# Groups of unused products between the first TensorE stages, and another order of polar work and decoding, in a linear-attention and two-layer expert kernel

## The chip, the cores and the metric

The kernel runs on one core of one Trainium2 chip. The metric is the time of one execution in device microseconds (us). TensorE (PE in the rows), VectorE (DVE), ScalarE (ACT), GpSimd (POOL) and the DMA queues each have a queue of their own, worked off in order. They meet at semaphores.

## What is computed

Three parts follow each other: a linear attention with a complex decay, a feed-forward layer with a leaky slope, and a layer of eight experts of which each token takes one.

```python
def _attn_ref(q, k, v, a_re, a_im):          # 4 batches, 8 heads, 768 steps, 48 channels
    mag = np.sqrt(a_re * a_re + a_im * a_im)
    scale = np.minimum(mag, 0.999) / (mag + 1e-06)
    ...
    for t in range(S):
        S_re, S_im = ar * S_re - ai * S_im + kv, ar * S_im + ai * S_re
        y[:, :, t] = np.einsum('bhd,bhde->bhe', q[:, :, t], S_re)

def _moe_ref(x, w_in, w_out, alpha):          # 3072 tokens, 384 -> 2048 -> 384
    h = x @ w_in
    g = np.maximum(h, 0.0) + alpha * np.minimum(h, 0.0)
    return g @ w_out

def _moe2_ref(x, modality_id, w_gate, modality_bias, w1, w2):
    e_idx = np.argmax(x @ w_gate + modality_bias[modality_id], axis=1)
    ...
    out[mask] = gate_w[mask, None] * (np.maximum(x[mask] @ w1[e], 0.0) @ w2[e])
```

## The kernel before

The 768 steps are cut into 6 chunks of 128, so that with 4 batches there are 24 pieces (`k`). Two pieces make a unit of 256 tokens (`u`), 12 units in all.

For each pair of pieces the polar work (`polar_group`, lines 673 to 789) turns the decays into magnitude and angle. VectorE and ScalarE share it: squares, reciprocal roots, an arctangent, running products and sums (line 737), sine and cosine, and at its end the tile `z`. The first pair runs as two halves, the second one (pieces 2 and 3) in one on tiles named `p`. `z` is written to memory and read back in another layout as `qk` (`bounce`, `bounce_back`). Then `attn` computes the products `pa`, masks them on VectorE into `at`, turns the keys (`pk`, copied by ScalarE into `ks`), forms `py` and the state sum `pu`, and splits `py` into a high part on ScalarE (`t`, `xt`, line 831) and a low part on VectorE (line 832). Two small DMAs per piece complete `xt`.

The feed-forward weights come as 64-bit numbers. `decode` (lines 613, 616, 619) puts them together on VectorE, three instructions for each of 16 blocks. ScalarE makes the high part of a block (line 566), VectorE the low part `w` (line 567), TensorE turns the block (`pl`, line 571) and ScalarE copies that to `wT`. `weights_gate` multiplies `wT` with the gate's weights (`og`, line 585), which ScalarE copies out as `of`.

`moe1` runs 8 steps for each unit. A step has 18 products into `ph` (lines 876 to 879), ScalarE's `n` (line 884), VectorE's `n` (line 886), ScalarE's `gh` (line 889), VectorE's `gl` (line 864), and 12 products into `acc` (line 919). From unit 2 on, each unit's polar work and attention are spread over the steps of the unit before.

The order of the work before and between the first steps is written out by hand in two texts. `START` holds what comes before the first step, `TURN` what each of the first 15 steps adds. In them `x` and `y` stand for one polar instruction of piece 0 or 1, `q` for one of pieces 2 and 3, `p` for one of the third pair; `A`, `a`, `B`, `C` for one part of the attention of piece 0, of piece 1, of unit 1 and of unit 2; `D` for the decoding of two blocks and `F` for what follows it; `b` and `c` for the bounces; `r` makes later decoding stand behind the last VectorE instruction so far; `w` is a group of 28 products that nothing reads (`warm`, line 180), issued while the first bounce is under way. Between `<` and `>` the VectorE instructions are chained. A scheduler then places the instructions of each engine, so that the texts set the queues but don't equal them.

Of the kernel before, what the change touches and what calls it, by code (L numbers as in the profile page):

```python
# [11 lines left out]
F32 = mybir.dt.float32  # L12
# [7 lines left out]
B, H, S, D = 4, 8, 768, 48  # L20
# [7 lines left out]
F2 = 8  # L28
# [6 lines left out]
NEARLY = 4  # L35
NFINAL = 3
NTRIP = 1
START = 'x2 y x2 y2 x y3 x2 y x2 y3 < x3 y x y x < x3 > x y > x2 < x4 y x b y6 r y5 < c w A2 a A > a A a2 < > q12 D q12 r q7 F q5 D d'
TURN = ('B', 'D2 > B F2 B2 D B3', 'B L D F3', '', 'D', 'D F p', '', 'F', '< p2 < p > p3', 'p3 < p3 > p > p11', 'p7', '', 'p4 < C3', 'C2 p C3 >2 s >', '')
GHB = 3  # L40
ATB = 2
LEAD = 3
# [12 lines left out]
WL = 5  # L55
WN = 28
BB = 1
OT = "xg"
OB = 4
HD = 4  # L60
# [38 lines left out]
class Emit:  # L99
    def __init__(self, ctx, tc, aps):  # L100
        self.ctx, self.tc, self.nc = ctx, tc, tc.nc
        self.__dict__.update(aps)
        self.ahead, self.loaded = {}, None
        self.raws, self.vs, self.zs, self.zd, self.queue = {}, {}, {}, {}, None
        self.behind = None
        self.nwarm = 0
        self.paced = self.sine = None
        self.pacing = True
        self.scattered = []
        self.free = {"pa": ["pa0", "pa1"], "pq": ["pq0", "pq1"]}  # L110
# [14 lines left out]
    def consts(self):  # L125
        nc, cp = self.nc, self.cp
        self.tiny = cp.tile([128, 1], F32, name="tiny")
        nc.vector.memset(self.tiny, 1e-25)
        warm = cp.tile([128, 1], F32, name="warm")
        nc.scalar.activation(warm, self.tiny, AF.Abs_reciprocal_sqrt)  # L130
        self.trig = cp.tile([128, 1], F32, name="trig")
        self.ident = cp.tile([128, 128], F32, name="ident")
# [42 lines left out]
    def warm(self, x, n):  # L175

        pt = self.ps.tile([128, 512], F32, name=f"warm{self.nwarm}", tag="acc", bufs=2)
        self.nwarm += 1
        for _ in range(n):
            self.nc.tensor.matmul(pt[:, :128], self.ident, x, start=True, stop=True)  # L180

    def route_consts(self):
        nc, cp, mp = self.nc, self.cp, self.mp
# [213 lines left out]
    def unit_out(self, nm, nt, ids, gate, acc):  # L397
        nc, qp = self.nc, self.qp
        for t in range(nt):
            ot = qp.tile([128, XW], F32, name=f"ot{nm}_{t}", tag=OT, bufs=OB)[:, :DM]  # L400
            nc.vector.tensor_scalar(ot, acc[t], gate[:, t:t + 1], None, ALU.mult)
# [273 lines left out]
    def polar_group(self, ks, wa, wq, work, inline):  # L675
# [90 lines left out]
        for i, k in enumerate(ks):  # L766
# [11 lines left out]
            if inline:  # L778
                self.bounce(k)
                if not BB:  # L780
                    self.bounce_back(k)
        if inline and BB:
            for k in ks:
# [376 lines left out]
def body(ctx, tc, aps):  # L1160
    em = Emit(ctx, tc, aps)
# [4 lines left out]
    def polar(*ks):  # L1166
        st = third if ks[0] == 4 else em.polar(ks)
        for k in ks:
            em.load_v(k)
        yield  # L1170
        yield from em.polar_run(st, 0, len(ks), True)
        yield

    def run(gen, n=1000):
        for _ in range(n):
            v = 1
            while v == 1:
                v = next(gen, 0)
            if v == 0:
                return  # L1180

    def op(gen):

        while next(gen, 1) != 1:
            pass
# [12 lines left out]
    def attn_unit(u):  # L1198
        xts[u] = em.wp.tile([128, 3, 2, 256], F32R, name=f"xt{u}", tag="xt", bufs=XB)
        for k in (2 * u, 2 * u + 1):  # L1200
            yield from em.attn(k, xts[u])
# [17 lines left out]
    def chained(c):  # L1219

        done = len(tc.nc.cur_bb.bb.instructions)
        with tc.issue_after(chain[0]) if chain[0] else nullcontext():
            step(c)
        for i in tc.nc.cur_bb.bb.instructions[done:]:
            if i.engine == mybir.EngineType.DVE:
                chain[0] = i

    def step(c):

        if c in "xyqp":  # L1230
            op(gens[c])
        elif c in "AaB":
            next(gens[c], 0)
        elif c == "w":
            em.warm(zs0[WZ][:, 0, 0, :CH], WN)
        elif c == "b":
            zs0[0] = em.zs[0]
            em.bounce(0)
            if BX:
                em.bounce_back(0)  # L1240
        elif c == "c":
            zs0[1] = em.zs[1]
            em.bounce(1)
            if not BX:
                em.bounce_back(0)
            em.bounce_back(1)
            em.weights_load(range(WL, 9 + W9))
            for k in (2, 3):
                em.load_v(k)
        elif c == "r":  # L1250
            em.behind = em.last
        elif c == "s":
            em.behind = None
        elif c == "C":
            run(gens["C"], 1)
        elif c == "L":
            for k in ("pa", "pq"):
                em.free[k].remove(k + "1")
        elif c == "d":
            em.weights_load(range(9 + W9, NFC))  # L1260
            third.extend(em.polar((4, 5)))
        elif c in "De":
            if not parts or parts[-1][1] == 0:
                if fc[0] == NFC:
                    return
                parts.append([em.weights_part(fc[0], fc[0] + 1), 1])
                fc[0] += 2
            while True:
                parts[-1][1] = next(parts[-1][0], 0) or 0
                if c == "e" or parts[-1][1] == 0:  # L1270
                    break
        elif c == "F":
            if parts:
                next(parts.pop(0)[0], 0)
# [3 lines left out]
    def steps(text):  # L1278

        for part in re.findall("([^0-9 ]+)([0-9]*)", text):  # L1280
            for c in part[0] * int(part[1] or 1):
                if c in "<>":
                    link[0] = c == "<"
                else:
                    with em.behind_turn() if c in PT else nullcontext():
                        (chained if link[0] else step)(c)

    gens["p"], gens["C"] = polar(4, 5), attn_unit(2)
    steps(START)
    jobs, later = {}, {}  # L1290
# [21 lines left out]

    for g, text in enumerate(TURN):
        first, _, then = text.partition("/")
# [74 lines left out]
    tab2, trip, n = tabs["f"]  # L1389
# [83 lines left out]
```

## Time and profile before

| | us |
|---|---|
| median of 3 runs | 902.87 |
| lowest and highest | 901.29 and 905.11 |
| the profiled execution, its own time | 901.13 |
| its span, from the first to the last instruction | 899.4 |
| TensorE, busy | 822.4 (91%) |
| VectorE, busy | 673.3 (75%) |
| ScalarE, busy | 466.6 (52%) |
| mean granted TensorE clock | 0.964 |

A time of the profile counts from the first instruction. A granted clock of 1.00 is TensorE at 2.4 GHz, 0.50 is 1.2 GHz. A row of the timeline gives the start, the time taken, the engine, the line and operation, the tiles written and read, the count, and in brackets how long the engine had been idle before it and what ended that. A row that takes longer than the step to the next row overlaps it, since an engine's instructions are pipelined.

### The profile page before, as it was taken

How to read it: one execution, taken by the hardware profiler on the slowest of the kernel's cores; microseconds unless marked ns; L12 is line 12 of the kernel's file. 1: busy time of each engine (PE TensorE's matmuls, PEld its weight loads, DVE VectorE, ACT ScalarE, POOL GpSimd, SP SyncE). 2: the span in 40 equal slices, each digit the busy share in tenths (PEclk: the TensorE clock that was granted, in tenths of full speed). 3: DMA queues.
4: the chain of work that ended last, by engine and by line, in shares of the span. 5: the costliest groups of instructions: out<-in, count | busy, mean ns of one | idle time of the engine just before them, and what ended most of it. 6: DMA issues, size and time to landing. Idle time of an engine off the chain costs nothing.

```text
span 899.4 us, 16054 instructions
## 1 busy us (share of the span) xinstructions
PE 822.4 (91%) x5949; PEld 783.4 (87%) x5949; DVE 673.3 (75%) x1419; ACT 466.6 (52%) x871; POOL 204.8 (23%) x204
## 2 busy tenths in 40 slices
PE   0769898999899999999999999899999999999893
PEld 0658898989899998999999999899988888999893
DVE  7999788999986978788888889355644755656851
ACT  7645266757564746565656464223343444455550
POOL 2000221021211121212121121000332543534650
PEclk9978698999999999999999999899999999999997
DMA  8869101645548235353626271500355477567650
GB/s 334 252 202 316 42 3 36 180 162 149 145 104 204 72 88 142 94 129 104 151 89 169 69 190 46 132 24 8 123 173 140 154 231 259 190 236 268 193 176 20
DMA packets 63591, 130.37 MB, mean 145 GB/s; under 512 B 10456, under 2 KB 39656, under 8 KB 63504
## 3 DMA queue, kind: packets, MB, share of 16 engines
q1 hardware_dynamic: 59536, 119.49, 44.4%
q0 software_dynamic: 3968, 9.77, 3.3%
q8 instruction: 49, 0.80, 0.4%
q14 instruction: 38, 0.31, 0.1%
HBM read 98.17 MB, written 28.91 MB: 141 GB/s over the span
## 4 chain that ended last, share of the span: by engine, by line
PE 61%; DVE 16%; DMA 8%; issue 4%; ACT 3%; POOL 1%; SPq 0%; DVEq 0%; ACTq 0%; POOLq 0%
PE acc L919 14%; PE a2s L505 6%; PE ph L876 6%; PE ph L879 5%; PE ph L877 5%; PE pa L807 4%; DMA zd<-z 3%; DMA qk<-zd 3%; PE p2s L490 2%; PE p2s L486 2%; PE p2s L487 2%; DVE n L886 2%; PE py L825 2%; PE pu L839 2%; PE og L585 1%
## 5 line engine op out<-in xcount | busy, mean ns | idle before, releaser
L876 PE MATMUL ph<-xt,w 128*128 128x256 f32 x576 | 157.0, 300 | 6.7 <-DVE n L886 4.2
L919 PE MATMUL acc<-w,gh 128*128 128x392 f32 x768 | 159.0, 345 | 0.4 <-ACT gh L889 0.4
L877 PE MATMUL ph<-xt,w 128*128 128x256 f32 x576 | 151.2, 290 | 0.0
L919 PEld LDWEIGHTS acc<-w,gh 128*128 128x128 f32 x768 | 134.0, 190 | 1.2 <-ACT gh L889 0.7
L876 PEld LDWEIGHTS ph<-xt,w 128*128 128x128 f32 x576 | 113.6, 197 | 8.8 <-DVE n L886 4.5
L886 DVE SCALAR_TENSOR_TENSOR n<-n,al,ph 128x256 f32<-128x256 f32 x192 | 83.9, 472 | 43.4 <-ACT n L884 42.9
L877 PEld LDWEIGHTS ph<-xt,w 128*128 128x128 f32 x576 | 113.8, 198 | 0.5 <-issue 0.5
L879 PE MATMUL ph<-xt,w 128*128 128x256 f32 x576 | 103.2, 289 | 0.0
L884 ACT ACTIVATE n<-ph 128x512 f32<-128x512 f32 x96 | 57.0, 593 | 74.8 <-PE ph L879 73.7
L864 DVE TENSOR_TENSOR gl<-n,gh 128x512 fp32r<-128x512 f32 x96 | 66.6, 694 | 33.5 <-ACT gh L889 33.4
L919 PE MATMUL acc<-w,gl 128*128 128x392 f32 x384 | 89.5, 348 | 0.0
L889 ACT CAST gh<-n 128x512 fp32r<-128x512 f32 x96 | 59.3, 617 | 57.2 <-DVE n L886 54.7
L879 PEld LDWEIGHTS ph<-xt,w 128*128 128x128 f32 x576 | 85.2, 196 | 0.0
L268 POOL DMA_INDIRECT tbl<-tok,ix x24 | 27.4, 1141 | 200.8 <-DVE ix L266 190.2
L919 PEld LDWEIGHTS acc<-w,gl 128*128 128x128 f32 x384 | 70.7, 193 | 0.3 <-issue 0.3
L807 PE MATMUL pa<-qk 96*128 96x128 f32 x384 | 54.0, 285 | 10.6 <-DMA qk<-zd 9.8
L807 PEld LDWEIGHTS pa<-qk 96*128 96x128 f32 x384 | 50.5, 197 | 13.3 <-issue 7.5
L494 DVE SCALAR_TENSOR_TENSOR hls<-p2s,hhs 128x512 fp32r<-128x512 f32 x32 | 22.0, 688 | 32.8 <-ACT hhs L493 32.8
L505 PE MATMUL a2s<-whs,hhs 128*128 128x384 f32 x128 | 43.8, 342 | 0.0
L505 PE MATMUL a2s<-wls,hhs 128*128 128x384 f32 x128 | 43.5, 340 | 0.0
L825 PE MATMUL py<-at,v 128*64 128x128 f32 x384 | 42.5, 289 | 0.3 <-DVE xt L832 0.3
L474 ACT CAST whs<-wrs 128x768 fp32r<-128x768 f32 x32 | 26.3, 834 | 30.8 <-PE a2s L505 17.0
(361 smaller groups left out, 1883.0 us busy)
## 6 DMA issues: line engine op xcount, KB each, us to landing
zd<-z SPq DMA_DIRECT2D x24, 771.0 KB, 4.7
qk<-zd SPq DMA_DIRECT2D x24, 771.0 KB, 7.2
wraw<-in_w_io_dram SPq DMA_DIRECT2D x16, 768.0 KB, 12.1
wrs<-in_wcat_dram SPq DMA_DIRECT2D x32, 384.0 KB, 4.2
ck<-in_w_io_dram SPq DMA_DIRECT2D x16, 768.0 KB, 5.0
wrf<-in_wcat_dram SPq DMA_DIRECT2D x24, 384.0 KB, 3.7
wa<-in_pa__dram SPq DMA_DIRECT2D x10, 768.0 KB, 4.8
wq<-in_pq__dram SPq DMA_DIRECT2D x10, 768.0 KB, 8.6
```

Source lines behind the costliest of these rows:

```text
L268: nc.gpsimd.indirect_dma_start(out=self.tbl, out_offset=bass.IndirectOffsetOnAxis(ap=ix, axis=0), in_=self.tok[:, c, b, :], in_offset=None ...
L505: nc.tensor.matmul(acc[t], x[:, 128 * t:128 * t + 128], w[:, DM:], start=(f == 0 and x is hh and w is wh), stop=(last and x is hl))
L807: nc.tensor.matmul(pa[:, i, :], kt[:, h, :], qt[:, h, :CH], start=True, stop=True)
L825: nc.tensor.matmul(o, v[:, h * D:h * D + 64], ats[g][:, i, :], start=True, stop=(c == 0))
L864: return engine.tensor_tensor(gl, nf, gh.bitcast(F32), ALU.subtract).ins
L876: nc.tensor.matmul(ph[:, i, :], w1(fc, 0, c), xt[:, c, 0, :], start=(c == 0), stop=False)
L877: nc.tensor.matmul(ph[:, i, :], w1(fc, 0, c), xt[:, c, 1, :], start=False, stop=False)
L879: last = nc.tensor.matmul(ph[:, i, :], w1(fc, 1, c), xt[:, c, 0, :], start=False, stop=(c == 2)).ins
L884: nc.scalar.activation(nf, ph, AF.Relu, scale=-1.0)
L886: paced = nc.vector.scalar_tensor_tensor(nf[:, i, :], nf[:, i, :], self.al1[:, 2 * p + i:2 * p + i + 1], ph[:, i, :], ALU.mult, ALU.add).ins
L889: copy = nc.scalar.copy(gh, nf).ins
L919: nc.tensor.matmul(acc[t][:, :XW], x[:, i, 128 * t:128 * t + 128], self.w[2 * p + i][:, h, DM:], start=(p == i == h == 0 and x is gh), sto ...
```

## The change

Two texts and one small function. `START` and `TURN` are written anew, and a step `f` is added: `fill` issues four products of the identity with itself into a buffer of the `acc` kind, directly behind the last TensorE instruction so far. Nothing reads them. `START` holds 11 such steps, that is 44 products. In the new `START` the second pair's polar work (`q`) begins between the halves of piece 1 and goes on in longer runs, the first decoding (`D`) stands behind most of it, and `r` stands behind the first part of the attention. In `TURN` the parts `D`, `F` and `p` of the first steps are regrouped, and the last two of unit 2's parts `C` move.

```diff
-START = 'x2 y x2 y2 x y3 x2 y x2 y3 < x3 y x y x < x3 > x y > x2 < x4 y x b y6 r y5 < c w A2 a A > a A a2 < > q12 D q12 r q7 F q5 D d'
-TURN = ('B', 'D2 > B F2 B2 D B3', 'B L D F3', '', 'D', 'D F p', '', 'F', '< p2 < p > p3', 'p3 < p3 > p > p11', 'p7', '', 'p4 < C3', 'C2 p C3 >2 s >', '')
+START = 'x3 y2 x3 y3 x y x y x y3 < x3 y2 x < x4 > x2 y > x3 < x y2 < x2 q b y10 c w A2 a A > r f a A f a f a < > q f2 q8 f2 q5 D F q3 r f q2 f q9 f q3 f q4 D d'
+TURN = ('B', 'D2 B F2 B > B2 D F B', 'B2 D F2 L', '', 'D', 'D F p', '', 'p3 F', '<2 p > p2', 'p > p3 < p3 > p11', 'p7', '', 'p4 < C3', 'C3 >2 s >', 'C p C')
...
+FN = 4
...
+    def fill(self, n):
+        if self.filled is None:
+            self.filled = self.ps.tile([128, 512], F32, name="fill", tag="acc", bufs=2)
+        last = [i for i in self.nc.cur_bb.bb.instructions if i.engine == mybir.EngineType.PE][-1]
+        with self.tc.issue_after(last):
+            for _ in range(n):
+                self.nc.tensor.matmul(self.filled[:, :128], self.ident, self.ident, start=True, stop=True)
...
+        elif c == "f":
+            em.fill(FN)
```

What the queues look like is seen in three places. On TensorE, at the end of piece 1's attention, where `pl` turns the first two decoded blocks and `ph_0` is the first step of unit 0, before:

```order
L825 MATMUL py_365<-at_0_316,v_135 64x128 x4
L825 MATMUL py_365<-at_1_346,v_135 64x128 x4
L571 MATMUL pl_447<-ident,wf_415 128x128 x3
L571 MATMUL pl_438<-ident,wf_414 128x128 x3
L876 MATMUL ph_0_514<-xt_151,w_435 128x256
```

and now:

```order
L836 MATMUL py_377<-at_1_354,v_135 64x128 x4
L191 MATMUL fill<-ident 128x128 x4
L850 MATMUL pu_397<-v_135,ks_1_361 96x48 x4
L191 MATMUL fill<-ident 128x128 x16
L582 MATMUL pl_455<-ident,wf_444 128x128 x3
L582 MATMUL pl_464<-ident,wf_445 128x128 x3
L191 MATMUL fill<-ident 128x128 x16
L887 MATMUL ph_0_559<-xt_151,w_452 128x256
```

Two blocks of 16 fills stand before and behind the two `pl`; the other 12 fills are in groups of 1 to 4 between the parts of the attention.

On VectorE, where piece 3's attention (`at_1`, `t_3`, `xt`, `state`) meets the decoding of the eighth pair of blocks, before:

```order
L809 TENSOR_TENSOR at_1_668<-pa_1_663,mask 128x512
L567 TENSOR_TENSOR w_751<-wf_560,w_751 128x768
L567 TENSOR_TENSOR w_759<-wf_561,w_759 128x768
L832 TENSOR_TENSOR t_3_686<-py_677,t_3_686 128x128
L613 TENSOR_SCALAR wf_743<-wraw_483 128x768
L613 TENSOR_SCALAR wf_744<-wraw_485 128x768
L832 TENSOR_TENSOR xt_499<-py_677,xt_499 128x3x128
L616 SCALAR_TENSOR_TENSOR wf_743<-wraw_483,wf_743 128x768
L616 SCALAR_TENSOR_TENSOR wf_744<-wraw_485,wf_744 128x768
L843 TENSOR_TENSOR state<-pu_733,qk_473 96x384
L619 SCALAR_TENSOR_TENSOR wf_743<-wraw_483,wf_743 128x768
```

and now:

```order
L820 TENSOR_TENSOR at_1_729<-pa_1_724,mask 128x512
L897 SCALAR_TENSOR_TENSOR n_1_770<-n_1_770,al_109,ph_1_738 128x256 x2
L875 TENSOR_TENSOR gl_0_776<-n_0_591,gh_0_595 128x512
L854 TENSOR_TENSOR state<-pu_794,qk_518 96x384
L843 TENSOR_TENSOR t_3_787<-py_778,t_3_787 128x128
L624 TENSOR_SCALAR wf_804<-wraw_528 128x768
L624 TENSOR_SCALAR wf_805<-wraw_530 128x768
L843 TENSOR_TENSOR xt_544<-py_778,xt_544 128x3x128
L627 SCALAR_TENSOR_TENSOR wf_804<-wraw_528,wf_804 128x768
L627 SCALAR_TENSOR_TENSOR wf_805<-wraw_530,wf_805 128x768
L630 SCALAR_TENSOR_TENSOR wf_804<-wraw_528,wf_804 128x768
```

`n_1` and `gl_0`, which stood ahead of `at_1`, stand behind it, the two `w` have gone ahead of it, and `state` has moved ahead of `t_3`. From the four `w` behind the last rows on, VectorE's queue is the same as before.

On ScalarE, where piece 2's `t_2` and `xt` are split off, before:

```order
L884 ACTIVATE n_1_725<-ph_1_693 128x512
L831 CAST t_2_624<-py_615 128x128
L566 CAST w_759<-wf_561 128x768
L831 CAST xt_499<-py_615 128x3x128
L587 COPY of_719<-og_712 128x16
```

and now:

```order
L895 ACTIVATE n_1_770<-ph_1_738 128x512
L577 CAST w_708<-wf_605 128x768
L577 CAST w_716<-wf_606 128x768
L842 CAST t_2_669<-py_660 128x128
L842 CAST xt_544<-py_660 128x3x128
```

Two `w` now stand between `n_1` and `t_2`. Lines after the change count 2 to 11 more than before; the first step of unit 1 (`ph_0` on `xt_499`, now `xt_544`) and all behind it on TensorE stand in the same order as before.

## Rows read from the trace of the kernel before

**Rows 1.** The page's part 1: busy us, share of the span, instructions of each engine.

```profile
PE 822.4 (91%) x5949; PEld 783.4 (87%) x5949; DVE 673.3 (75%) x1419; ACT 466.6 (52%) x871; POOL 204.8 (23%) x204
```

**Rows 2.** Busy time by stretch: stretch, us, each engine's busy us (instructions), TensorE's granted clock, DMA share, GB/s.

```profile
36.00:48.00 12.00, 10.25 (x103) 9.11 (x103) 12.00 (x17) 7.80 (x13) 0.00 (x0) 1.00 1.04 359
48.00:56.00 8.00, 2.54 (x23) 1.70 (x20) 8.00 (x12) 4.48 (x13) 0.00 (x0) 0.77 0.31 100
56.00:66.00 10.00, 7.29 (x40) 6.77 (x40) 10.00 (x19) 2.46 (x7) 0.36 (x2) 0.67 0.69 216
...
86.00:95.00 9.00, 8.87 (x50) 7.54 (x51) 5.41 (x10) 3.04 (x7) 0.00 (x0) 0.62 0.14 42
95.00:110.00 15.00, 12.51 (x67) 11.43 (x66) 10.49 (x17) 4.38 (x12) 2.84 (x11) 0.67 0.25 52
110.00:130.00 20.00, 19.43 (x144) 19.11 (x144) 17.91 (x29) 11.70 (x23) 6.04 (x8) 0.99 0.05 11
```

**Rows 3.** Timeline of VectorE.

```profile
28.43 0.95 DVE L687 TENSOR_TENSOR p<-p,p 128x768 f32<-128x768 f32 x1
...
59.88 1.02 DVE L613 TENSOR_SCALAR wf<-wraw 128x768 int32<-128x768 int32 x2
...
70.81 0.69 DVE L809 TENSOR_TENSOR at<-pa,mask 128x512 f32<-128x512 f32 x1 [0.37 <-PE pa L807]
...
88.52 0.69 DVE L809 TENSOR_TENSOR at<-pa,mask 128x512 f32<-128x512 f32 x1 [1.78 <-PE pa L807]
...
92.75 0.29 DVE L832 TENSOR_TENSOR t<-py,t 128x128 fp32r<-128x128 f32 x1 [1.81 <-ACT t L831]
...
97.27 0.55 DVE L843 TENSOR_TENSOR state<-pu,qk 96x384 f32<-96x384 f32 x1 [1.09 <-PE pu L839]
...
99.47 3.56 DVE L567 TENSOR_TENSOR w<-wf,w 128x768 fp32r<-128x768 f32 x4
...
104.33 0.55 DVE L613 TENSOR_SCALAR wf<-wraw 128x768 int32<-128x768 int32 x1
108.30 0.99 DVE L864 TENSOR_TENSOR gl<-n,gh 128x512 fp32r<-128x512 f32 x1 [3.42 <-ACT gh L889]
```

**Rows 4.** Timeline of TensorE.

```profile
27.73 8.45 PE L180 MATMUL warm<-z,ident 128*128 128x128 f32 x56 [27.73 <-DVE z L776]
...
52.89 0.87 PE L571 MATMUL pl<-ident,wf 128*128 128x128 f32 x3 [3.50 <-DVE xt L832]
55.72 0.55 PE L876 MATMUL ph<-xt,w 128*128 128x256 f32 x1 [1.95 <-DMA xt<-t]
...
59.45 1.40 PE L585 MATMUL og<-wg,wT 128*128 128x8 f32 x12
63.56 0.90 PE L571 MATMUL pl<-ident,wf 128*128 128x128 f32 x3 [2.71 <-DVE wf L619]
...
67.19 2.69 PE L919 MATMUL acc<-w,gh 128*128 128x392 f32 x8 [0.45 <-ACT gh L889]
...
83.89 0.55 PE L571 MATMUL pl<-ident,wf 128*128 128x128 f32 x3 [0.57 <-ACT wT L575]
...
101.38 2.73 PE L585 MATMUL og<-wg,wT 128*128 128x8 f32 x12 [0.57 <-ACT wT L575]
104.43 2.73 PE L585 MATMUL og<-wg,wT 128*128 128x8 f32 x12 [0.32 <-ACT of L587]
107.01 0.56 PE L876 MATMUL ph<-xt,w 128*128 128x256 f32 x1
...
148.97 0.58 PE L876 MATMUL ph<-xt,w 128*128 128x256 f32 x1 [4.15 <-DVE n L886]
```

**Rows 5.** Timeline of ScalarE.

```profile
68.74 1.70 ACT L566 CAST w<-wf 128x768 fp32r<-128x768 f32 x2 [1.60 <-DVE wf L619]
```

**Rows 6.** Busy time of TensorE in single microseconds of the warm group.

```profile
29.00:30.00 1.00, 1.00 (x7) 1.00 0.71 290
...
34.00:35.00 1.00, 1.00 (x11) 1.00 1.19 232
```

More of the change, by code (lines that the diff above doesn't have):

```diff
@@ L106, in __init__ @@
         self.nwarm = 0
+        self.filled = None
         self.paced = self.sine = None
```

## Prediction

> **What bounds the kernel now.** I read four views in this order. The page first: TensorE is busy 91% of the span [rows 1], so for most of the 899 us the kernel goes at TensorE's pace, and a change that touches only the first 110 us can bring no more than an earlier entry into that long stretch. Then the busy time by stretch, which shows that the first 110 us are another regime: from 36 to 66 us VectorE is busy in every microsecond (12.00 of 12, 8.00 of 8, 10.00 of 10), while TensorE has 2.54 us of work in the 8 us from 48 and its granted clock falls to 0.77 and 0.67; from 86 to 110 it stands at 0.62 and 0.67, and from 110 on at 0.99 with TensorE busy 19.43 of 20 us [rows 2]. Third, VectorE's timeline: where it waits at all between 30 and 110 us (0.37, 1.78, 1.81, 1.09, 3.42 us [rows 3]) and for whom. Last, TensorE's timeline: where it has nothing to do and what its instructions then cost. The same group of 12 `og` rows takes 1.40 us at 59.45 and 2.73 us at 101.38 and 104.43, the first just after the clock was back at 2.4 GHz, the others at 1.2 GHz [rows 4].
>
> So there are two gates. Up to some 86 us VectorE's queue sets the pace. From 86 to 107 VectorE and TensorE wait for each other, TensorE mostly at 1.2 GHz. At 107.01 the first step of unit 1 starts, from there on TensorE's order is unchanged and it is the bound until 148.97, where it waits 4.15 us for a VectorE `n` [rows 4]. I therefore sum the change up to two marks behind which the order is the old one: `ph` at 107.01 on TensorE, and `gl` at 108.30 on VectorE.
>
> **Start to 60 us: equal.** The polar and decoding instructions are the same ones in another order, and a queue without a wait ends at the same time in any order. One polar instruction of pieces 2 and 3 now stands ahead of the end of piece 1's `z`. It starts at 28.43 and 0.87 us later the next follows [rows 3], so `z` is later by 0.87 us, and with it the warm group, the second write of the bounce and the read of `qk` that is queued behind it on the DMA queue. VectorE has `q` steps to fill that. I count 0, with 0 and +0.9 as ends.
>
> **The fills.** 44 products are added. The warm group's products have the same shape: 11 rows a microsecond in its fast part, 7 in its slow part [rows 6], two rows to a product (28 products are 56 rows [rows 4]), so 0.18 and 0.29 us each. 16 of them cost 2.9 or 4.6 us. The first block of 16 lies where TensorE now has 3.50 us of idle time before 52.89 [rows 4]; free. The second stands between the second `pl` and the first step. `pl` waits for decoding, which now stands behind most of the polar work. The pair's `z` ended at 59.88, where the next decoding began [rows 3], and ends there still; behind the two blocks' decoding stand now one polar product and two `w` of 0.87 us each and eight half-wide products for `z` of some 0.47, 6.4 us, so it ends at 53.5, with small latencies at 53.9. So `pl` ends at 54.3, the fills at 57.2, and `ph` starts there instead of at 55.72, 1.5 us late. But before, TensorE had sat idle and ran the 18 products of this step at 1.2 GHz, from 55.72 to 59.45 [rows 4]; at 2.4 GHz they take half of these 3.7 us, some 2, to 59.2. So the fills cost nothing at the end of the step, if they hold the clock; and behind it lies the 2.71 us wait for decoding before 63.56 [rows 4], which VectorE sets. Sum: 0. At 1.2 GHz they would cost 1.7 us more plus the slow step; that is a rival below.
>
> The Trainium skill's page "TensorE: Matmul & The Clock Gate" says in "What's actually happening" that the low clock is the default and activity lifts it. The trace agrees: 0.77 follows the emptiest stretch, and 0.99 the fullest [rows 2]. [...]
>
> **60 to 86 us: a small loss.** At 63.56 TensorE again comes out of idle time, as before, and I expect it to run at 1.2 GHz again: the group of 8 `acc` rows at 67.19 takes 2.69 us [rows 4]. So the mask `at` of piece 2 waits as now, 0.37 us [rows 3]. On ScalarE two `w` stand ahead of `t_2` now; a pair takes 1.70 us [rows 5]. One of them stood between `t_2` and its `xt` before, and VectorE arrives at `t_2` some 0.8 us after `n_1` is out, so about half of the pair shows: I take a new wait of 0.85 us, ends 0 and 1.7.
>
> **86 to 100 us: three waits go.** VectorE waited 1.78 us for `pa`, since four `pl` in a row each waited 0.57 us for a copy ahead of it [rows 4]; now the `pl` are spread between products that are ready. It waited 1.81 us for `t_3`, whose products stood behind a slow `acc`; now `n_1`, `gl_0` and `state` stand there as work. It waited 1.09 us for `pu`, which now stands ahead of `py` on TensorE. Together 4.68 us [rows 3]. Less 0.85 makes 3.8: the four `w` that start at 99.47 start at about 95.7. What is late next is TensorE: `pl` of the last two decoded blocks, then two `og` groups, with a ScalarE copy between them.
>
> **The two marks.** From the four `w` to the end of the row at 104.33, VectorE needs 5.4 us (104.88 less 99.47), so it arrives at `gl` at 101.1. There it waited 3.42 us for ScalarE's `gh`, which stood behind the copies of the two `og` [rows 3, 4]. With both `og` at 1.40 us, they start at 96.3, when the last `pl` is through behind the decoding that ends as the four `w` begin, and end at 99.4 (1.40, the 0.3 us between the two rows, 1.40); `gl` could follow 1.1 us behind that, as 108.30 follows the end of the second group at 107.16, which is before VectorE arrives: 101.1, 7.2 us earlier. With both at 2.73 us they end at 102.1, `ph` of unit 1 starts there (4.9 us earlier) and `gl` at 103.2: 5.1 us earlier. I lean to the slow one: `og` products are tiny and stand behind waits for decoding now as before, and before exactly that stretch fell to 1.2 GHz. **Forecast: 5 us earlier at both marks.** From there to the end the order is unchanged, TensorE and VectorE arrive equally early, and the later bounces, which are released by them, move along. So 901.13 less 5 gives 896.1 against the profiled execution. The median of the runs shown lies 1.7 us above that execution; I take half of that and predict 897.0.
>
> **Rivals.**
>
> *The clock holds through 110 us.* For it: VectorE's waits go, so TensorE has fewer holes from 78 to 88. Then 7.2 us at `gl`, and TensorE gains another 1.5 us as the `ph` and `acc` behind 107.01 run at full speed. 7 to 9 us: 892 to 894 against the profiled execution, 894 to 896 against the median.
>
> *The clock falls again from 88 to 95 and at the `og` too.* `pu`'s and `og`'s small products at 83 to 86, then 2 us or so of waiting for `at_1` of piece 3, which stands behind the decoding. Then the fourth step's 18 products and 12 others take 6 us instead of 3, and `og` the slow time: both marks only 2.3 us earlier, less if `t_2` costs 1.7. 0 to 4 us: 897 to 901 against the profiled execution, 899 to 903 against the median. This rests on the rows alone: at 83.89 a run of short groups with 0.57 us of idle time between them, and 0.62 as the clock of the stretch behind [rows 2, 4].
>
> The skill's same page, in "A second HAM failure mode: psum-queue depth-cycling", tells of such short idle times between groups of products that let the clock go up and down. The trace agrees with it at 83.89; by it alone this rival would come before the forecast.
>
> *Slower: the second block of 16 fills runs at 1.2 GHz.* The place is between the second `pl` and `ph` of unit 0, the point from which it decides the clock at 54 us. If TensorE's 1 us of waiting for the decoding there lets the clock drop, the 16 fills take 4.6 us, `ph` starts at 59, runs 3.7 us at the slow clock and its `og` 2.73, to 65.5 instead of 60.85. The wait before 63.56 takes up 2.7 of these 4.6 us; the rest delays the gate's copies on ScalarE, with them `gh`, `acc`, `pa` and `at`, by 2 us. With the clock then low through the stretch from 86 as in the rival before, and `t_2` at its dear end, the three waits that went return as others: 1 to 6 us slower, 904 to 909 against the median. Against it: TensorE is fed with 16 fills before, too.
>
> *The change does nothing*, since something not moved sets both marks. Only the DMAs of `xt` could, and they are issued when VectorE has written `xt`, which moves with it. It is in the 0 to 4 us.
>
> **How the numbers follow.** Chances: forecast (4 to 7 us) 0.50, the clock holds 0.15, little gain 0.25, slower 0.10. The range runs from the best of the second case by the profiled execution, 892.0, to 902.0, three quarters through the little gain by the median; it leaves out the slower case and that last quarter, some 0.16. About 0.5%, 4.5 us, is what a measurement of this kernel can tell from no change; against the median that is 898.4. Faster by more: all of the second case and three quarters of the forecast, 0.52. Slower by more: half of the last, 0.05. Within: 0.43.
>
> **What would show it.** Right: the granted clock from 48 to 60 us at 1.00; `ph` of unit 0 at 57 and its `og` ending near 61; VectorE's waits of 1.78, 1.81 and 1.09 us gone and the four `w` at 95 to 96; `ph` of unit 1 at 101 to 103, `gl` with little or no wait; the wait of some 4 us before 148.97 still there, 5 us earlier. Wrong: a clock of 0.5 at 54 to 60 (then the slower rival), a wait of more than 1 us at VectorE's `t_2` or at `at_1` of piece 3, `og` groups of 2.73 us together with slow `ph` from 88 on (little gain), or marks that are 5 us early but a later bounce or `n` that gives it back.

## The result, and the profile after

| | before | after |
|---|---|---|
| median, runs beside each other, us | 902.93 (901.29 to 905.11, 4 runs) | 892.62 (891.09 to 894.00, 4 runs) |
| ratio of the times, 95% interval | | 0.9888 (0.9863 to 0.9914) |
| the profiled execution, its own time, us | 901.13 | 894.0 |
| its span, us | 899.4 | 892.2 |
| mean granted TensorE clock | 0.964 | 0.979 |

The kernel is 10.3 us faster. 897.0 was predicted, 892.0 to 902.0 the range: right in sign and inside the range, but near its lower end. The two profiled executions are only 7.2 us apart in span: the one of before took 1.8 us less than its median, the one of after 1.4 us more. In two later sets of runs (below), each beside the kernel before on one chip, the changed kernel was 7.2 us faster (892.46 against 899.70, ratio 0.9926) and 8.5 us faster (894.67 against 903.15, 0.9916). The three intervals of the ratio overlap, and 10.3 us is the highest of the three distances.

The page's part 1 (busy us, share, instructions) of the changed kernel:

```profile
PE 821.8 (92%) x6037; PEld 784.8 (88%) x6037; DVE 669.9 (75%) x1419; ACT 467.2 (52%) x871; POOL 205.2 (23%) x204
```

TensorE's busy time is that of before [rows 1], with 88 rows more: 44 products of two rows.

Busy time by stretch (us, each engine's busy us with its instructions, granted clock, DMA share, GB/s), the stretches of [rows 2] without the first, and with the one from 66 to 86:

```profile
48.00:56.00 8.00, 8.00 (x84) 7.78 (x83) 7.89 (x13) 4.30 (x9) 0.00 (x0) 1.00 0.34 112
56.00:66.00 10.00, 8.46 (x72) 7.96 (x70) 10.00 (x19) 3.66 (x10) 1.68 (x2) 1.00 0.69 224
66.00:86.00 20.00, 19.00 (x166) 17.03 (x166) 20.00 (x29) 10.36 (x22) 1.54 (x1) 1.00 1.04 368
86.00:95.00 9.00, 7.58 (x51) 7.07 (x51) 9.00 (x15) 4.26 (x9) 0.99 (x2) 0.81 0.24 59
95.00:110.00 15.00, 14.96 (x92) 14.62 (x90) 14.73 (x24) 7.45 (x18) 6.78 (x16) 0.77 0.20 30
110.00:130.00 20.00, 19.43 (x143) 19.15 (x143) 15.72 (x23) 12.72 (x25) 3.00 (x4) 1.00 0.01 1
```

The kernel before in the stretch that [rows 2] leaves out:

```profile
66.00:86.00 20.00, 17.70 (x141) 15.79 (x140) 19.63 (x29) 10.61 (x24) 1.78 (x2) 0.92 1.03 352
```

Two things differ from before, and they must be kept apart. The clock holds at 1.00 from 48 to 86 us, where it was 0.77, 0.67 and 0.92. And VectorE is busy for 9.00 of the 9 us from 86 (5.41 before) and 14.73 of the 15 from 95 (10.49).

VectorE's timeline at the instructions that waited in [rows 3], and at the four `w` and the `gl` that were the mark:

```profile
69.71 0.69 DVE L820 TENSOR_TENSOR at<-pa,mask 128x512 f32<-128x512 f32 x1
...
78.79 0.30 DVE L843 TENSOR_TENSOR t<-py,t 128x128 fp32r<-128x128 f32 x1
...
86.66 0.70 DVE L820 TENSOR_TENSOR at<-pa,mask 128x512 f32<-128x512 f32 x1
...
88.64 0.57 DVE L854 TENSOR_TENSOR state<-pu,qk 96x384 f32<-96x384 f32 x1
89.11 0.30 DVE L843 TENSOR_TENSOR t<-py,t 128x128 fp32r<-128x128 f32 x1
...
94.18 3.58 DVE L578 TENSOR_TENSOR w<-wf,w 128x768 fp32r<-128x768 f32 x4
...
99.88 0.98 DVE L875 TENSOR_TENSOR gl<-n,gh 128x512 fp32r<-128x512 f32 x1 [0.27 <-ACT gh L900]
```

None of the rows up to the four `w` has a bracket, which stands for an idle time: no wait is left there. The four `w` start 5.3 us earlier than in [rows 3] (99.47), `gl` 8.4 us earlier (108.30), and its own wait has shrunk from 3.42 to 0.27 us.

TensorE's timeline: the two blocks of fills, the places of [rows 4], and a wait behind the change:

```profile
51.24 3.80 PE L191 MATMUL fill<-ident 128*128 128x128 f32 x32
54.88 0.82 PE L582 MATMUL pl<-ident,wf 128*128 128x128 f32 x6
55.54 3.74 PE L191 MATMUL fill<-ident 128*128 128x128 f32 x32
59.03 0.36 PE L887 MATMUL ph<-xt,w 128*128 128x256 f32 x1
...
61.24 1.40 PE L596 MATMUL og<-wg,wT 128*128 128x8 f32 x12
63.89 0.52 PE L582 MATMUL pl<-ident,wf 128*128 128x128 f32 x3 [1.25 <-DVE wf L630]
...
66.29 1.69 PE L930 MATMUL acc<-w,gh 128*128 128x392 f32 x8 [0.32 <-ACT gh L900]
...
94.91 1.40 PE L596 MATMUL og<-wg,wT 128*128 128x8 f32 x12
...
96.63 2.11 PE L596 MATMUL og<-wg,wT 128*128 128x8 f32 x12
98.60 0.58 PE L887 MATMUL ph<-xt,w 128*128 128x256 f32 x1
...
141.54 0.45 PE L887 MATMUL ph<-xt,w 128*128 128x256 f32 x1 [4.15 <-DVE n L897]
```

The `og` that took 2.73 us twice [rows 4] takes 1.40 and 2.11. Unit 1's first `ph` starts at 98.60 instead of 107.01. The wait of 4.15 us for `n` is still there, 7.4 us earlier.

### The profile page after: what moved, and what is told of

Its sections match the earlier page's. It is cut to its first block, busy times and chain, and to the rows that moved or that the text cites. A ratio compares the mean times of both kernels' runs of the same rounds, so it can differ in the third digit from the quotient of the medians.

```text
span 892.2 us, 16224 instructions
## 1 busy us (share of the span) xinstructions
PE 821.8 (92%) x6037; PEld 784.8 (88%) x6037; DVE 669.9 (75%) x1419; ACT 467.2 (52%) x871; POOL 205.2 (23%) x204
## 4 chain that ended last, share of the span: by engine, by line
PE 53%; DVE 22%; DMA 12%; issue 6%; ACT 3%; POOL 2%; SPq 1%; POOLq 0%; ACTq 0%; DVEq 0%
PE acc L930 12%; PE a2s L516 6%; DMA qk<-zd 6%; PE ph L887 5%; PE ph L888 4%; PE ph L890 4%; PE pa L818 3%; DVE n L897 2%; PE p2s L501 2%; PE p2s L497 2%; PE p2s L498 2%; DMA zd<-z 2%; DVE z L785 2%; PE pu L850 2%; PE py L836 2%
## 5 line engine op out<-in xcount | busy, mean ns | idle before, releaser
L887 PE MATMUL ph<-xt,w 128*128 128x256 f32 x576 | 153.8, 295 | 5.2 <-DVE n L897 4.2
L888 PE MATMUL ph<-xt,w 128*128 128x256 f32 x576 | 148.0, 285 | 0.0
L887 PEld LDWEIGHTS ph<-xt,w 128*128 128x128 f32 x576 | 110.9, 192 | 7.1 <-DVE n L897 4.8
L888 PEld LDWEIGHTS ph<-xt,w 128*128 128x128 f32 x576 | 111.1, 193 | 0.2 <-issue 0.2
L890 PE MATMUL ph<-xt,w 128*128 128x256 f32 x576 | 102.1, 286 | 0.0
L890 PEld LDWEIGHTS ph<-xt,w 128*128 128x128 f32 x576 | 83.5, 192 | 0.0
L818 PE MATMUL pa<-qk 96*128 96x128 f32 x384 | 54.3, 285 | 13.6 <-DMA qk<-zd 11.7
```

What stands on the lines that cost most here:

```text
L818: nc.tensor.matmul(pa[:, i, :], kt[:, h, :], qt[:, h, :CH], start=True, stop=True)
L887: nc.tensor.matmul(ph[:, i, :], w1(fc, 0, c), xt[:, c, 0, :], start=(c == 0), stop=False)
L888: nc.tensor.matmul(ph[:, i, :], w1(fc, 0, c), xt[:, c, 1, :], start=False, stop=False)
L890: last = nc.tensor.matmul(ph[:, i, :], w1(fc, 1, c), xt[:, c, 0, :], start=False, stop=(c == 2)).ins
```

## The experiments

Theory: the gain comes from the order on VectorE between 76 and 99 us, that is from `TURN`. First rival: it comes from the fills, by the clock. Second rival: it comes from the new `START`. The first four kernels take the change apart; all ran on one chip, where the kernel before took 901.7 us.

**Changed kernel without the fills** (no `f` in `START`):

```diff
-... r f a A f a f a < > q f2 q8 f2 q5 D F q3 r f q2 f q9 f q3 f q4 D d
+... r a A a a < > q q8 q5 D F q3 r q2 q9 q3 q4 D d
```

> The changed kernel without its 44 fills; the queues of VectorE and ScalarE are the same but for a few neighbours. Theory A (the order makes the gain: VectorE no longer waits between 86 and 100 us, the fills only change the clock where VectorE sets the pace): 8 to 10 us faster than the kernel before still, less at most 1; TensorE at 1.2 GHz from about 52 and at 63 to 70, VectorE without a wait above 0.5 us up to the four w. Theory B (the fills make it: the clock they hold keeps TensorE ahead of VectorE up to 86): the clock falls at 52 and stays low to 70, VectorE gets waits of 0.5 to 2.5 us each at the masks, and the gain falls to 3 to 5 us.

895.14 us, ratio 0.9939 (0.9915 to 0.9964). Its clock falls as in the kernel before (0.86, 0.67 and 0.88 in the three stretches from 48 to 86), VectorE has a wait of 1.01 us for `pa` at 71.57 us, and `gl` starts at 102.25 us. More than half of the gain is there without a fill: 6.6 us, less than the 8 to 10 of theory A and more than the 3 to 5 of theory B. The wait of 1.01 us is one that theory A had excluded.

**Kernel before with 44 fills**, everything else old:

```diff
-... c w A2 a A > a A a2 < > q12 D q12 r q7 F q5 D d
+... c w A2 a A > f a A f a f a f < > q12 f2 D q12 f2 r q7 f F q5 f D f d
```

> The kernel before with 44 fills at the places that answer to the changed kernel's, and nothing else. Theory A: no change, within 1.5 us of the kernel before; the clock stays at 1.00 from 48 to 60, but VectorE's waits of 1.78, 1.81 and 1.09 us between 86 and 98 stay. Theory B: 5 us faster or more, with the clock at 1.00 up to about 80 and some of the three waits gone.

900.87 us, ratio 0.9986 (0.9961 to 1.0011): no difference that can be told. The fills do their work on the clock, as the stretches show (0.77 and 0.67 before):

```profile
48.00:56.00 8.00, 8.00 (x83) 7.77 (x82) 8.00 (x12) 3.42 (x10) 0.00 (x0) 1.00 0.34 109
56.00:66.00 10.00, 8.66 (x71) 8.39 (x71) 10.00 (x19) 4.35 (x11) 1.41 (x2) 0.93 0.53 173
```

and VectorE's timeline shows that the waits of [rows 3] are still there, 4.18 us together instead of 4.68:

```profile
89.11 0.69 DVE L820 TENSOR_TENSOR at<-pa,mask 128x512 f32<-128x512 f32 x1 [2.15 <-PE pa L818]
92.87 0.29 DVE L843 TENSOR_TENSOR t<-py,t 128x128 fp32r<-128x128 f32 x1 [1.34 <-ACT t L842]
...
96.98 0.55 DVE L854 TENSOR_TENSOR state<-pu,qk 96x384 f32<-96x384 f32 x1 [0.69 <-PE pu L850]
```

`gl` starts at 106.59 in this execution, 1.7 us earlier than in [rows 3], and the first of the two `og` takes 1.57 us there. Of that the medians show 0.8 us, which is inside the interval.

**Changed kernel with the old `TURN`** (new `START` and fills stay):

```diff
-TURN = ('B', 'D2 B F2 B > B2 D F B', 'B2 D F2 L', ...
+TURN = ('B', 'D2 > B F2 B2 D B3', 'B L D F3', ...
```

> The changed kernel with the old TURN: new START with its fills, old order of decoding between the first steps. Theory A: the three waits of VectorE stay, some 4.7 us together, so 0 to 3 us faster than the kernel before. Theory B: 6 us faster or more, the clock alone keeps the waits small.

900.95 us, ratio 0.9999 (0.9975 to 1.0023): no difference that can be told, though `gl` starts at 105.69, 2.6 us earlier than before. VectorE's three waits are half of what theory A expected: 0.57, 1.09 and 0.68 us. The start of `pa` behind the bounce shows where the 2.6 us went in this execution. TensorE's timeline, first of this kernel, then of the kernel before:

```profile
245.54 1.86 PE L818 MATMUL pa<-qk 96*128 96x128 f32 x7 [5.19 <-DMA qk<-zd]
```

```profile
246.10 1.19 PE L807 MATMUL pa<-qk 96*128 96x128 f32 x7 [3.16 <-DMA qk<-zd]
```

VectorE ended the `z` for it 2.6 us earlier (its last part at 232.54 instead of 235.13), but the bounce through memory took 13.0 us instead of 11.0, so 2.0 of the 2.6 us became a longer wait. That compares two single executions, and 11.0 us is the shortest bounce of all (last section); it does not explain the medians, whose interval leaves room for a gain of some 2 us.

**Kernel before with the new `TURN`**, old `START`, no fills:

```diff
-TURN = ('B', 'D2 > B F2 B2 D B3', 'B L D F3', ...
+TURN = ('B', 'D2 B F2 B > B2 D F B', 'B2 D F2 L', ...
```

> The kernel before with the new TURN alone: no fill, old START. Theory A: VectorE's three waits between 86 and 98 go, 4 to 8 us faster than the kernel before. Theory B: the clock at 0.5 from 52 and from 62 as before, 0 to 3 us faster.

892.50 us, ratio 0.9902 (0.9879 to 0.9924): all of the gain, and more than the 4 to 8 us that theory A gave, with the clock as low up to 66 us as before (0.79 and 0.67). Both rivals fall as the main cause. Only the second and third step of `TURN` matter: in a program with these two alone, which was built but not timed, the order on TensorE, VectorE, GpSimd and the DMA queues is the same as with all of `TURN`, and ScalarE's differs by one pair of small instructions.

**One half of the two steps each.** They differ in two things: where the chain `>` ends, and how the parts are grouped.

```diff
-'D2 > B F2 B2 D B3', 'B L D F3'
+'D2 B F2 B > B2 D B2', 'B L D F3'
```

> The kernel before with one half of the new TURN: in its second step the chain is ended later and the decoding of the sixth pair stands behind the attention's first part. On VectorE the first mask (at_0) of piece 3 then stands ahead of the decoding of the seventh pair of blocks instead of behind it, and n, gl stand behind at_1, as in the new order; the two w stay behind t_3 and state stays late. No fills, old START. Theory (each of the moves takes out its own wait, the first mask the one of 1.78 us for pa): that wait goes, a wait of 1 to 2 us at t_3 stays since only n and gl (1.5 us) stand between at_1 and t_3, four w at 96 to 97.5 instead of 99.47, time 895 to 899. Rival (the two w ahead of at_1 carry the gain): no gain, within 2 us of the kernel before. Rival (the first mask carries all of it): as with the whole new TURN, 891 to 894.

897.54 us against 899.7 of the kernel before on that chip, ratio 0.9979 (0.9960 to 0.9999).

```diff
-'D2 > B F2 B2 D B3', 'B L D F3'
+'D2 > B F2 B2 D F B2', 'B2 D F2 L'
```

> The kernel before with the other half of the new TURN: the parts of the attention, of F and of D are regrouped over the second and third step, but the chain ends where it did. On VectorE the two w and n, gl and state come ahead of at_1; both masks of piece 3 stay behind the decoding of the seventh pair. No fills, old START. Theory (each of the moves takes out its own wait): the wait for pa at at_1 goes, since w, n, gl and state (4.5 us) stand ahead of it, but t_3 comes two instructions behind at_1 and waits 2 to 3 us, four w at 97 to 98, time 897 to 901. Rival (the w carry the gain): four w at 94 to 95, time 891 to 894.

894.53 us, ratio 0.9941 (0.9915 to 0.9967). Each half seems to give a part: the chain as much as was expected of it, the regrouping 2.5 us more. The times alone don't prove it: the chain's interval ends just short of no change, and the regrouping's overlaps that of the whole change on this chip (0.9926, 0.9899 to 0.9954). That neither half is the whole rests on the timelines: four `w` and `gl` start at 94.18 and 99.88 us in the changed kernel (95.28 and 100.95 in its second execution), later in both halves. VectorE's timeline, first of the chain alone, then of the regrouping alone:

```profile
88.68 0.29 DVE L832 TENSOR_TENSOR t<-py,t 128x128 fp32r<-128x128 f32 x1 [0.98 <-ACT t L831]
...
92.34 0.56 DVE L843 TENSOR_TENSOR state<-pu,qk 96x384 f32<-96x384 f32 x1 [0.38 <-PE pu L839]
...
96.76 3.55 DVE L567 TENSOR_TENSOR w<-wf,w 128x768 fp32r<-128x768 f32 x4
...
105.66 0.99 DVE L864 TENSOR_TENSOR gl<-n,gh 128x512 fp32r<-128x512 f32 x1 [3.50 <-ACT gh L889]
```

```profile
93.19 0.29 DVE L832 TENSOR_TENSOR t<-py,t 128x128 fp32r<-128x128 f32 x1 [0.95 <-ACT t L831]
96.47 3.61 DVE L567 TENSOR_TENSOR w<-wf,w 128x768 fp32r<-128x768 f32 x4
...
103.60 0.80 DVE L864 TENSOR_TENSOR gl<-n,gh 128x512 fp32r<-128x512 f32 x1 [1.67 <-ACT gh L889]
```

The wait of 1.78 us at `at` is gone in both, and the wait at `t` is down to about 1 us, less than was expected. The four `w` start almost equally early, 2.7 and 3.0 us before [rows 3]. But `gl` is 2.6 us earlier in the one and 4.7 in the other, because of the two `og` ahead of it on TensorE. Chain alone:

```profile
98.74 2.73 PE L585 MATMUL og<-wg,wT 128*128 128x8 f32 x12 [0.57 <-ACT wT L575]
101.79 2.73 PE L585 MATMUL og<-wg,wT 128*128 128x8 f32 x12 [0.32 <-ACT of L587]
```

Regrouping alone:

```profile
98.41 1.50 PE L585 MATMUL og<-wg,wT 128*128 128x8 f32 x12
100.74 1.72 PE L585 MATMUL og<-wg,wT 128*128 128x8 f32 x12
```

With the chain alone TensorE still goes into the `og` through waits (1.63 us ahead of the `pl` before them, 0.57, 0.32) and the granted clock is 0.66 from 95 to 110; with the regrouping it has no idle time there and the clock is 0.89.

**The changed kernel again**, beside these two:

> The changed kernel itself once more, beside the others on one chip. Theory (the new TURN makes the gain, fills and new START together add nothing): 892 to 893, ratio 0.988 to 0.992, the same as the kernel with the new TURN alone (892.5, ratio 0.9902). Rival (the fills bring a gain on top, by the granted clock from 50 to 87 us): 890 or less, ratio under 0.987.

892.46 us, ratio 0.9926 (0.9899 to 0.9954), where the kernel before took 899.7 us. This time its clock fell to 0.93 from 66 to 86 and to 0.62 from 86 to 95, `gl` started at 100.95, and the time is the same. The rival, a gain of the fills on top, did not come.

**An attempt on the wait of 4.15 us** that TensorE keeps at `ph` at 141.5 us:

```diff
-'p > p3 < p3 > p11', 'p7'
+'p > p3 < p3 > p8', 'p10'
```

> The changed kernel, and in addition the long run of 11 polar instructions of the third pair in the tenth step is cut to 8, the other 3 go to the eleventh. On VectorE the second half of an n (of the sixth step of unit 0) then stands ahead of the running sums over x and s instead of behind five of them (4.3 us). It goes for the wait of 4.15 us that TensorE has at ph at 141.5 us in the changed kernel. Theory (TensorE is the bound again behind this ph): the wait falls to under 0.5 us, gl's wait of 1.89 us at 149.3 us goes, ph and all behind it come 2 to 4 us earlier, time 889 to 891. Rival (VectorE's polar work sets the bounce that pa waits for at 238.8 us, so what TensorE gains is given back there): the wait of 5.06 us there grows by as much as the other shrinks, time 892 to 893.

895.46 us, ratio 0.9948 (0.9926 to 0.9969): no gain, and by the medians 3 us behind the changed kernel beside it, though the two intervals overlap. Both expectations fell. The wait did not go, it moved to the next `ph`, and others came behind it. TensorE's timeline:

```profile
146.69 0.35 PE L887 MATMUL ph<-xt,w 128*128 128x256 f32 x1 [3.41 <-DVE n L897]
186.61 1.54 PE L850 MATMUL pu<-v,ks 128*96 128x48 f32 x16 [2.03 <-DVE xt L843]
```

The polar work that was taken from one `n` came to stand ahead of the next one. `pa` behind the bounce, which waits for VectorE's last `z`, started at 241.75 us, 1.2 to 3.0 us later than in the changed kernel's three executions (238.76 to 240.53). As far as one attempt tells, VectorE sets the pace here too, and moving its instructions about doesn't shorten its queue.

**Four kernels on one chip, all with the new `TURN`**: old or new `START`, with or without fills. The first is the kernel with the new `TURN` alone plus the fills as above; the second and third ran before under other names.

> One of four kernels on one chip that all have the new TURN: START old or new, fills without or with. This one: old START with 44 fills put into it (12 between the parts of the attention, 24 ahead of the first pl, 8 behind the second). Theory (VectorE sets the pace up to 100 us, so that the clock of TensorE there is worth nothing as long as the two og near 95 us run at full speed): 891 to 894, the same as old START without fills. Rival (the fills take 3 us off, as the distance from the new START without them to the changed kernel suggests): 888 to 890.

> Second of the four: old START, no fills, new TURN; the same kernel that ran at 892.5 (ratio 0.9902). Theory: 891 to 894, the same as the changed kernel. Rival: 3 us slower than the first of the four.

> Third of the four: new START, no fills, new TURN; the same kernel that ran at 895.14 (ratio 0.9939). Theory: between 892 and 896, at most 3 us slower than the changed kernel: without the fills the masks wait 1.6 us in sum up to 72 us, as they showed in its first profile. Rival (the new START is worth its own gain): faster than old START without fills.

> Fourth of the four: the changed kernel. Theory: 892 to 893, within 1.5 us of old START without fills. Rival: 2 us or more faster than old START without fills.

| `START` | fills | median, us | ratio to before (903.15), 95% interval | mean clock of the runs |
|---|---|---|---|---|
| old | yes | 894.54 | 0.9913 (0.9881 to 0.9945) | 0.978 |
| old | no | 893.36 | 0.9902 (0.9874 to 0.9930) | 0.970 |
| new | no | 895.31 | 0.9916 (0.9882 to 0.9949) | 0.969 |
| new | yes (the changed kernel) | 894.67 | 0.9916 (0.9886 to 0.9947) | 0.975 |

The four are the same within what can be told, and none of the four rivals came; the first and the fourth lie just above the range that theory gave them. In the first set the new `START` without fills had been 2.6 us behind the new `TURN` alone (895.14 and 892.50); here it is 2.0 behind it and 0.6 behind the changed kernel, and the intervals overlap, so a cost of the new `START` is neither shown nor excluded. The fills raise the mean granted clock by 0.006 to 0.008 and buy nothing that can be measured in the times. In single traces they are not quite nothing: with the old `START`, VectorE's wait at `at` near 71 us (0.63 and 0.45 us in the two executions without fills) is gone with them, and `gl` starts at 100.03 instead of 100.87 and 100.98; with the new one at 99.53 to 100.95 instead of 101.20 and 102.25. So a gain of a microsecond or two by the fills, less than these intervals can tell, is not excluded.

## Why the prediction was right, point by point

*Start to 60 us, equal.* Held: VectorE's rows show no wait from 26 to 99.9 us. The decoding that began at 59.88 [rows 3] begins at 60.11, so this term is 0.2, inside the 0 to 0.9 of the prediction.

*The fills, 0.* Held, with two sizes off. A block of 16 products took 3.74 us where 2.9 was estimated from the warm group [rows 6]: 0.117 us a row against 0.09. And the first block was not free. It took 3.80 us from 51.24 on, so that `pl` started at 54.88, though the two blocks had been decoded at 53.84; 53.9 was predicted. So `ph` of unit 0 started at 59.03 and its `og` ended at 62.64, not at 57.2 and 60.85. The wait for decoding behind it, 2.71 us in [rows 4], took that up as said and is 1.25 us now. Two readings ahead of this sum were wrong. The microsecond with 7 rows has a granted clock of 1.00 [rows 6], so the dear price, 4.6 us a block, was no price at 1.2 GHz, and no run shows one. And [rows 2] don't show the highest clock in the fullest stretch: from 86 to 95 TensorE was busy 8.87 of 9.00 us at 0.62.

*60 to 86 us, a loss of 0.85.* The first step that failed. It rested on two readings. The clock was to fall again: it stayed at 1.00, `acc` took 1.69 us instead of 2.69, and the 0.37 us at `at` went. And `t_2` was to wait behind the pair of `w` on ScalarE, half of which was to show: it doesn't wait. ScalarE's timeline of the changed kernel:

```profile
76.33 0.60 ACT L895 ACTIVATE n<-ph 128x512 f32<-128x512 f32 x1 [0.32 <-PE ph L890]
76.82 1.55 ACT L577 CAST w<-wf 128x768 fp32r<-128x768 f32 x2
78.28 0.27 ACT L842 CAST t<-py 128x128 fp32r<-128x128 f32 x1
```

VectorE comes to `t_2` at 78.79, 1.9 us after `n` was out (76.93), not 0.8, and `n` begins 1.2 us earlier than before (77.52). Measured: 0.4 us gained instead of 0.85 lost.

*86 to 100 us, three waits of 4.68 us go.* Right, all three. With the 0.37 us above that is 5.05 us; 5.3 was measured at the four `w`, where 3.8 was forecast. (The four `pl` in a row that the prediction names had waited 0.26 us once and 0.57 three times.)

*The two marks.* The second step that failed, and the largest: "I lean to the slow one". Both `og` were to take 2.73 us again, since they are tiny and stand behind waits. One took 1.40 and the other 2.11; in the seven further executions with the whole new `TURN` and nothing else in it the second took 1.50 to 1.65. So the slow `og` of before was no property of `og`: it went when the idle time ahead of it (0.57, 0.32 us and what VectorE's three waits left on TensorE) went, and of the two halves the one that leaves idle time there keeps it. Idle time directly ahead is not all, though. In all eight executions with the new `TURN` the clock fell again between 97 and 102 us, with TensorE busy 0.96 or more of every microsecond from 91 on; the `og` came before that fall or ran into its start. Single microseconds of TensorE there (as in [rows 6]):

```profile
96.00:97.00 1.00, 0.96 (x8) 1.00 0.00 2
97.00:98.00 1.00, 1.00 (x9) 0.67 0.39 139
98.00:99.00 1.00, 1.00 (x6) 0.50 0.00 0
```

Why it fell there stays open. The prediction had the arithmetic for this case, `gl` at 101.1; it was given as a rival with 0.15. Measured: 8.4 us at `gl` and at `ph` of unit 1, where 5.1 and 4.9 were forecast. The rival's condition, that the clock holds through 110 us, was only half met: it is 0.81 and 0.77 from 86 on, and in the next execution of the same kernel it was 0.62 and 0.89.

*Carried to the end unchanged.* Not quite. Of the 8.4 us, 7.4 are left at the `ph` behind the 4.15 us wait. Then `z` for the bounce at 225 us is 9.2 us earlier, but `pa` behind it starts at 238.76, 7.3 us earlier (246.10 before, shown above), and from there to the end both executions take the same (653.3 and 653.4 us). The last part of that `z` on VectorE, before and now, and the `pa` now:

```profile
235.13 0.55 DVE L776 TENSOR_TENSOR z<-wq,x 128x384 f32<-128x384 f32 x1
```

```profile
225.89 0.55 DVE L787 TENSOR_TENSOR z<-wq,x 128x384 f32<-128x384 f32 x1
```

```profile
238.76 2.08 PE L818 MATMUL pa<-qk 96*128 96x128 f32 x8 [5.06 <-DMA qk<-zd]
```

The bounce, from the start of that part to `pa`, took 12.9 us against 11.0. It took 11.7 to 13.0 us in the twelve other profiled executions, the kernel before with fills among them: the 11.0 of the profile of before is the odd one. An estimate: with 12.5 us that execution would have been 1.5 us longer, at 902.6, which is the median of before. That is the likely cause of the 7.2 us between the traces against the 10.3 between the medians, together with the 1.4 us on the other side; with one trace of the kernel before it isn't shown. The 7.2 and 8.5 us of the two later sets also put 10.3 us at the upper end of the gain. The predicted 897.0 stood for a gain of 5.9 us; by all three measurements that was too small.

*The slower rival* (fills at 1.2 GHz) had its condition unmet: the clock was 1.00 from 48 to 66. *Little gain*, which by the Trainium skill's page "TensorE: Matmul & The Clock Gate" (section "A second HAM failure mode: psum-queue depth-cycling": short idle times between groups of products let the clock swing) would have come first, had its condition half met. The trace agrees as far as the clock goes: 0.62 to 0.81 from 86 to 95 in all kernels with the new `TURN`. But it cost no time that shows, and VectorE was busy in each of these 9 us.

In sum: the mechanism (three waits of VectorE go, TensorE enters unit 1 earlier, the order behind it stays) was right. The size was off by two terms. The stretch from 60 to 86 us was 1.2 us too dear (0.4 gained instead of 0.85 lost), and the two `og` at the slow clock 2.1 us by the prediction's own sum (7.2 less 5.1). Together that is the 3.3 us by which `gl` came earlier than forecast. The median fell inside the range only because the range reached down to the rival in which the clock holds, and that rival's condition was half met.

## What to carry to other kernels

Before work is added to keep TensorE's clock up, look at which engine is busy in every microsecond of the stretch; where it is another, the clock can rise, as here from 0.67 to 1.00, without a gain that the times show. An engine's waits are worth removing in the order in which they come, since the wait of a second engine (here TensorE's idle time ahead of `og`, and its slow clock) can be the echo of the first one's. And a wait that is removed on a full queue can move to the next consumer, as the one at 141 us did, when the queue gets no shorter.

## What was not expected of the hardware

The time of one and the same kernel follows its mean granted clock from run to run: 25 runs of the kernel before on one chip lie between 904.78 us at 0.959 and 895.64 us at 0.974, with a correlation of -0.92 and some 0.6 us for each 0.001. Between kernels that line doesn't hold: the kernel before with fills had 0.973 in the mean and took 900.87 us, the kernel with the new `TURN` alone 0.970 and 892.50 us. So here the mean clock of a kernel did not tell whether it was faster. The reading that fits is that a low clock costs time only where TensorE sets the pace.

The bounce through memory (from the last `z` to the `pa` behind it) took between 11.0 and 13.0 us in the 14 profiled executions, and the time from that `pa` to the end between 650.6 and 654.7 us. Why is not shown; a difference of 2 us between two single traces of this kernel is within that.
